# Windowed attention followed by routed expert attention on one Trainium2 core: the last row block in two halves, an earlier first key cast, and branch hints for five engines

## The chip, the core and the metric

The kernel runs on one core of a Trainium2 chip. A core has a TensorE that multiplies matrices (PE in the profile, with PEld for its weight loads), a VectorE (DVE), a ScalarE (ACT), a GpSimd (POOL) and a SyncE (SP) that here only issues transfers. Each engine works through its own instructions strictly in program order and waits on semaphores for the others. The metric is the device time in microseconds; lower is better.

## What is computed

The reference chains two layers. The first is attention with 4 batches, 8 heads, 768 positions and a head size of 64, in which a row sees the 8 first keys and the 96 last ones, with a bias that falls with distance. The second takes its output as x (4 × 768 × 512) and runs 4 causal attention experts of size 64; each row adds up its two best experts.

```python
    keep = is_global | is_local
    scores = scores + bias[None, :, :, :]
    scores = np.where(keep, scores, -1000000000.0)
    ...
    logits = x @ w_gate
    topk = np.argpartition(-logits, K, axis=-1)[..., :K]
    ...
    for e in range(E):
        ...
        ye = a @ v @ wo[e]
        for kk in range(K):
            mask = topk[:, :, kk] == e
            out += mask[..., None] * w[:, :, kk:kk + 1] * ye
```

## The kernel before, in words

The work is cut into 24 units of 128 rows (NU = 24, six per batch). The order of everything is written out by hand: ORDER (lines 791 to 830) is a string of slots such as `kc0v`, which means stage `kc` of unit 0 on engine v. The loop at lines 765 to 769 calls the stages in that order, so each slot puts its instructions at the end of its engine's queue. The last letter names the engine that does the copy or issues the transfer: a for ScalarE, g for GpSimd, v for VectorE, s for SyncE.

For one unit, the stages are these. `lk`, `lq`, `lv` load 256 KB of keys, queries and values in float32 (line 238), each kind into six rotating buffers. `kc`, `qc` cast them to float16 (line 258), and `vc`, `vx` cast the values (line 267). `tk`, `tq` transpose keys and queries on TensorE (line 283), with a copy out of PSUM (line 285). `sa`, `sb` make the local scores: a matmul first puts the bias from `biasT` into PSUM (line 345), another adds the scores (line 352), and ScalarE takes the exponential (line 355). `gs`, `vg`, `va`, `vb` are the scores of the eight first keys and the sums over values (lines 323, 366, 381). `tx` turns the result, `pk`, `pq`, `pv` project it for the experts (lines 414, 428), and `ro` is one step of the routing. `ca`, `cb`, `cc` are the experts' scores with their exponentials (lines 459, 462), and `ma` masks the diagonal block on GpSimd (line 474). `za` and `zb` sum over values for experts 0, 1 and 2, 3 (line 487); after `zb`, VectorE makes the reciprocal, the routing factor and the scaled result `zs` for all four experts (lines 494, 496, 498). `tz` turns `zs` (line 509, copy at line 512), and `ou` multiplies by `wo`, copies the 128 × 512 result to `osb` and stores it (lines 519, 522, 523).

`wm` slots are matmuls on the identity whose result nobody reads (line 248, 128 × 240 each); they stand where TensorE would idle. `xb` (lines 84 to 95) makes the constants of the local bias on VectorE: nine instructions, of which the last four write `biasT`. `ck` (lines 741, 742) counts, on VectorE, how many reciprocals of row sums lie in the allowed range. At the end the counts are summed by one matmul (line 774), reduced and made an integer on VectorE (lines 776, 778), and read by all engines (line 780); a branch (line 782) goes to a general path if a count is short. `bh` marks that branch for a prefetch hint on three engines.

PSUM has three pools here: `psS` (tag s, two buffers), `psZ` (tag z, one buffer) and `psT` (tag t, two buffers). A tile of a tag takes the buffers of that tag in turn and has to wait until the buffer's last reader is through. In the kernel before, the tiles of `tz` and `ou` and the count `nps` are all of tag t, and the score tiles `sps`, `gps`, `vgps`, `cps` are of tag s.

Of the kernel before, what the change touches and what calls it, by code (L numbers as in the profile page):

```python
# [18 lines left out]
P = 128  # L19
# [3 lines left out]
def kernel(  # L23
# [27 lines left out]
    NU = B * NT  # L51
    NH = 3
    HG = H // 2
    VW = Dh + 1
    sc1 = 1.0 / float(Dh) ** 0.5
    sc2 = 1.0 / float(Hd) ** 0.5
    slopes = [2.0 ** (-8.0 * (h + 1) / H) for h in range(H)]


    const = ctx.enter_context(tc.tile_pool(name="const", bufs=1))  # L60
    ident = const.tile([P, P], F16)
# [4 lines left out]
    biasT = const.tile([P, NP, W], F16)  # L66
    ident2 = const.tile([P, KB], F16)
    rel = const.tile([P, W], F32)
# [12 lines left out]
    col_i = const.tile([P, P], I32)  # L81
    G.iota(col_i[:, :], pattern=[[1, P]], channel_multiplier=0, base=0)

    def bias_constants(_):
        V.tensor_copy(rel[:, :], rel_i[:, :])
        ge = const.tile([P, W], F32, name="ge")
        V.tensor_scalar(ge[:, :], rel[:, :], 0.0, None, op0=Alu.is_ge)
        lt = const.tile([P, W], F32, name="lt")
        V.scalar_tensor_tensor(lt[:, :], rel[:, :], float(NL), ge[:, :],
                               op0=Alu.is_lt, op1=Alu.mult)  # L90
        V.tensor_scalar(lt[:, :], lt[:, :], -1.0, -NEG, op0=Alu.add, op1=Alu.mult)
        V.tensor_scalar(rel[KB:P, :], rel[KB:P, :], slopes[1] / slopes[0], None, op0=Alu.mult)
        for p in range(NP):
            V.scalar_tensor_tensor(biasT[:, p, :], rel[:, :], -slopes[2 * p] / sc1, lt[:, :],
                                   op0=Alu.mult, op1=Alu.add)

    def half_identities(_, on):
        for r in (slice(0, KB), slice(KB, P)):
# [44 lines left out]
    rinv2 = const.tile([P, B, NT, E], F32)  # L143
# [5 lines left out]
    wo16 = const.tile([P, NEP, D], F16)  # L149
# [41 lines left out]
    pp = fast.enter_context(tc.tile_pool(name="pp", bufs=3))  # L191
    psS = fast.enter_context(tc.tile_pool(name="psS", bufs=2, space=PSUM))
    psZ = fast.enter_context(tc.tile_pool(name="psZ", bufs=1, space=PSUM))
    psT = fast.enter_context(tc.tile_pool(name="psT", bufs=2, space=PSUM))
# [22 lines left out]
    def held(name, u):  # L217
        t, n, owner = rings[name]
        assert owner[u % n] == u
        return t[:, u % n]  # L220
# [9 lines left out]


    fs, kqT, kgs, vgs, ags, xTs, kqs, lgs, wts, a2s, as_, done = ({} for _ in range(12))
    s16s, zs_, x16s, routing, zss, zts, tps, ppss, zs2 = ({} for _ in range(9))

    def load(u, nm, on):
        b, ri = divmod(u, NT)
# [240 lines left out]
    def causal_values(u, i):  # L477

        b, ri = divmod(u, NT)
        n, a2 = ri + 1, a2s[u]  # L480
        assert done["m", u]
        if i == 0:
            zs2[u] = current["z"] = psZ.tile([P, 2, 4 * P], F32, name="zps2", tag="z")
        z_ps = zs2[u][:, 0, 0:E * VW].rearrange("r (e d) -> r e d", e=E)
        for e in range(i * E // 2, (i + 1) * E // 2):
            for ci in range(n):
                mm(z_ps[:, e, :], lhsT=a2[:, e % 2, (e // 2) * n + ci, :],  # L487
                   rhs=held("v2buf", b * NT + ci)[:, e, :], start=(e == 0 and ci == 0), stop=True,
                   skip_group_check=True)
        if i == 0:  # L490
            return
        assert next(routing[u // NH], "end") == "end"
        rinv = rinv2[:, b, ri, :]
        V.reciprocal(rinv, z_ps[:, :, Hd])
        ce = pp.tile([P, E], F32, name="ce")
        V.tensor_mul(ce[:, :], rinv, wts[u // NH][:, ri % NH, :])
        zss[u] = pp.tile([P, E, Hd], F16, name="zs")
        V.tensor_tensor(zss[u][:, :, :], z_ps[:, :, 0:Hd],  # L498
                        ce[:, :].unsqueeze(2).to_broadcast([P, E, Hd]), op=Alu.mult)

    def turn_z(u, on):
        zts[u] = pp.tile([P, NEP, P], F16, name="zt")
        if on == "s":
            nc.sync.dma_start_transpose(zts[u][:, :, :],
                                        zss[u][:, :, :].rearrange("r e d -> r (e d)"))
            return
        zt_ps = psT.tile([P, NEP, P], F16, name="ztps", tag="t")
        for ep in range(NEP):
            nc.tensor.transpose(zt_ps[:, ep, :],  # L509
                                zss[u][:, 2 * ep:2 * ep + 2, :].rearrange("r e d -> r (e d)"),  # L510
                                ident[:, :])
        copies[on](zts[u][:, :, :], zt_ps[:, :, :])  # L512

    def output(u, on):
        b, ri = divmod(u, NT)
        assert 3 in ready
        o_ps = psT.tile([P, D], F32, name="ops", tag="t")
        for ep in range(NEP):
            mm(o_ps[:, :], lhsT=zts[u][:, ep, :], rhs=wo16[:, ep, :],  # L519
               start=(ep == 0), stop=(ep == NEP - 1))  # L520
        o_sb = pp.tile([P, D], F32, name="osb", bufs=6)
        copies[on](o_sb[:, :], o_ps[:, :])
        dma(out[b, ri * P:(ri + 1) * P, :], o_sb[:, :])

    def top_two(pool, lg, wt, nm, n):

# [218 lines left out]
    def branch_hint(_):  # L745

        tc.mark_branch_hint_location("general", hint="LikelyTaken", engines=(
            mybir.EngineType.PE, mybir.EngineType.Activation, mybir.EngineType.DVE))

    stages = {  # L750
        "lk": (load, "k"), "lq": (load, "q"), "lv": (load, "v"),
        "kc": (cast, "k"), "qc": (cast, "q"), "vc": (cast_v, 0), "vx": (cast_v, 1),
        "wi": (weights_in,), "wc": (weights_cast,), "gi": (global_keys,),
        "vs": (select_values,), "xb": (bias_constants,), "xi": (half_identities,),
        "xm": (global_mask,), "xc": (global_bias,), "xk": (key_mask,), "xs": (selection,),
        "az": (local_zeros,), "xt": (act_tables,), "wm": (keep_warm,),
        "tk": (turn, 0), "tq": (turn, 1), "sa": (local_scores, 0), "sb": (local_scores, 1),
        "gs": (global_scores,), "vg": (global_values,),
        "va": (local_values, 0), "vb": (local_values, 1), "tx": (turn_x,),
        "pk": (project_qk, 0), "pq": (project_qk, 1), "pv": (project_v,), "ro": (route,),  # L760
        "ca": (causal_scores, 0), "cb": (causal_scores, 1), "cc": (causal_scores, 2),
        "ma": (causal_mask,), "za": (causal_values, 0), "zb": (causal_values, 1),
        "tz": (turn_z,), "ou": (output,), "ck": (check_sums,), "bh": (branch_hint,),
    }
    for slot in ORDER.split():
        stage, *args = stages[slot[:2]]
        if slot[-1].isalpha():
            args.append(slot[-1])
        stage(int(slot[2:].rstrip("agsv")), *args)
# [2 lines left out]
    V.memset(ones[:, :], 1.0)  # L772
    n_ps = psT.tile([1, NCHK], F32, name="nps", tag="t")
    mm(n_ps[:, :], lhsT=ones[:, :], rhs=good[:, :], start=True, stop=True)
    n_f = const.tile([1, 1], F32)
    V.reduce_sum(n_f[:, :], n_ps[:, :], axis=Ax.X)
    n_i = const.tile([1, 1], I32)
    V.tensor_copy(n_i[:, :], n_f[:, :])
    total = P * B * NT * (H + E)
    n_ok = nc.values_load(n_i[0:1, 0:1], min_val=0, max_val=total)  # L780
    fast.close()
# [7 lines left out]


ORDER = """
xb0 lk0s kc0v lq0s az0v az1g lk1s xi0a xs0v xk0g lq1a wm14 tk0 qc0g lv0s kc1g lk2s lq2s lk3a
wm5 tq0a lq3s xc0g lv1a lv2s lq4s lk4a qc1v lq5s vc0g vx0g wm4 tk1 tq1v xm0v lk5s wm10 sa0 sb0
wm10 vs0 gi0 wi0a wm2 gs0 lk6s kc2v qc2v tk2 tq2v wm3 gs1 lq6s wm7 vg0 kc3g va0 vb0 vc1g vx1v
qc3a sa1 az2g sb1 tk3 tq3v tx0v wi1a vg1 az3g qc4a vc2g kc4g vx2v wm2 va1 wm4 sa2 sb2 vb1 qc5g
gs2 kc5a wc0g tk4 tq4v tx1v az4v lv3s vg2 va2 lv4s vb2 sa3 sb3 tk5 tq5v wm6 tx2v kc6a lq7s wi2a
qc6v wm4 sa4 sa5 tk6 vc3g tq6v pk0 sb4 sb5 wc1v pk1 wm2 gs3 wm2 pq0a vx3v pq1a gi1 vg3 vc4g
vx4g wi4s lv5s va3 vb3 lk7a ca0 ma0 pk2 pq2v tx3v ca1 vg4 va4 vb4 lq8s ca2 pk3 pq3a lk8s vc5v
vx5v cb2 vg5 wc2g lv6s kc7g lq9s pv0v pv1v lq10a lk9s qc7g qc8g kc8g ca3 cb3 tk7 lv7s tq7v pv2v
ro0 va5 sa6 tk8 tq8v tx4v vc6g vx6g lk10a lk11s vb5 sb6 gs4 lv8s ro0 pv3v pk4 qc9g pq4v ro0 ro0  # L800
# [24 lines left out]
vb23 cc17 ma16 tz15v pk21 pq21a za16 ro6 zb16 tx22v ro6 ca19 ca20 ma17 tx23v ma18 ma19 za17  # L825
tz16v zb17 ou14a pv21v cb20 ca21 za18 pv22v pv23v ro7 zb18 cb21 pk22 ro7 ro7 ro7 pq22a ma20
ma21 pk23 pq23a ro7 za19 zb19 ca22 ou15v tz17v cb22 za20 cc22 tz18v ro7 ro7 ou16a zb20 ou17v
ck0 ck1 ca23 bh0 cb23 za21 tz19v zb21 ou18v cc23 tz20v ma22 za22 zb22 tz21a ou19a ou20v ma23 za23 tz22v
zb23 ou21a ou22a tz23v ou23a ck2
"""  # L830

MAXB = 512
# [38 lines left out]
```

## Time and profile before

| what | us |
|---|---|
| median of the three runs | 152.31 |
| lowest and highest run | 150.82, 152.47 |
| the profiled execution's own time | 152.97 |
| its span, first to last instruction | 150.8 |
| TensorE busy in the span | 140.3 (93%) |
| VectorE, ScalarE, GpSimd busy | 111.4, 108.1, 90.2 |
| data moved | 27.77 MB, mean 184 GB/s |

The profiled execution took 152.97 us, of which 150.8 us lie between its first and last instruction, and some 2.2 us around them. Busy TensorE is not TensorE at its peak, because matmuls are pipelined and their ends are modelled. The page cuts the span into 40 slices of 3.77 us; each digit is a busy share in tenths. The chain is followed back from the last work instruction to whatever released each step.

### The profile page before, as it was taken

How to read it: one execution, taken by the hardware profiler on the slowest of the kernel's cores; microseconds unless marked ns; L12 is line 12 of the kernel's file. 1: busy time of each engine (PE TensorE's matmuls, PEld its weight loads, DVE VectorE, ACT ScalarE, POOL GpSimd, SP SyncE). 2: the span in 40 equal slices, each digit the busy share in tenths (PEclk: the TensorE clock that was granted, in tenths of full speed). 3: DMA queues.
4: the chain of work that ended last, by engine and by line, in shares of the span. 5: the costliest groups of instructions: out<-in, count | busy, mean ns of one | idle time of the engine just before them, and what ended most of it. 6: DMA issues, size and time to landing. Idle time of an engine off the chain costs nothing.

```text
span 150.8 us, 7217 instructions
## 1 busy us (share of the span) xinstructions
PE 140.3 (93%) x3029; PEld 110.2 (73%) x3029; DVE 111.4 (74%) x348; ACT 108.1 (72%) x176; POOL 90.2 (60%) x254
## 2 busy tenths in 40 slices
PE   5799999999999999999978999999999999999760
PEld 4567778887778888878757778888778878786520
DVE  4838676687899887878863987687787777778850
ACT  4027657778576888888638998887977978989640
POOL 7278351568878988797827899136286345463200
PEclk9999999999999999999999999999999999999999
DMA  4999998999999989899899963415221005013462
GB/s 99 280 252 286 276 261 192 254 247 238 277 282 275 245 201 249 189 256 208 231 240 288 301 166 113 116 43 142 74 77 70 4 19 195 24 51 127 155 263 97
DMA packets 85364, 27.77 MB, mean 184 GB/s; under 512 B 82000, under 2 KB 82000, under 8 KB 85328
## 3 DMA queue, kind: packets, MB, share of 16 engines
q1 hardware_dynamic: 62496, 21.51, 56.6%
q10 hardware_dynamic: 22832, 5.77, 17.1%
q8 instruction: 24, 0.39, 1.0%
q14 instruction: 12, 0.10, 0.2%
HBM read 20.98 MB, written 6.29 MB: 181 GB/s over the span
## 4 chain that ended last, share of the span: by engine, by line
PE 74%; DMA 11%; DVE 4%; POOL 3%; ACT 2%; issue 1%; SPq 1%; ACTq 0%; POOLq 0%; DVEq 0%
PE pps L414 14%; PE cps L459 7%; PE vps L428 7%; PE tp L283 7%; PE ops L519 6%; PE zps L487 6%; PE zps L381 6%; PE sps L345 5%; PE zps L248 4%; DMA kf<-in_k_dram 4%; DMA vf<-in_v_dram 4%; PE xps L402 3%; PE sps L352 3%; DMA qf<-in_q_dram 3%; PE zps L366 2%; PE ztps L509 2%
## 5 line engine op out<-in xcount | busy, mean ns | idle before, releaser
L462 ACT ACTIVATE a<-cps 128x1024 f16<-128x1024 f32 (+1 forms) x48 | 42.2, 917 | 8.3 <-PE cps L459 6.6
L355 ACT ACTIVATE abuf<-sps 128x636 f16<-128x636 f32 (+1 forms) x48 | 30.6, 686 | 12.8 <-PE sps L352 10.1
L267 POOL CAST vbuf<-vf 64x256 f16<-64x256 f32 x76 | 31.0, 408 | 8.4 <-DMA vf<-in_v_dram 5.2
L474 POOL TENSOR_SCALAR_AFFINE_SELECT a<-a 128x256 f16<-128x256 f16 x48 | 18.3, 409 | 5.1 <-ACT a L462 4.8
L285 DVE COPY kqT<-tp 128x1024 f16<-128x1024 f16 x23 | 15.7, 688 | 6.6 <-PE tp L283 6.1
L390 DVE TENSOR_TENSOR x<-zps,rinv 128x512 f16<-128x512 f32 x24 | 16.6, 691 | 0.8
L487 PE MATMUL zps<-v2buf,a 128*128 128x65 f16 x336 | 16.0, 193 | 0.6 <-DVE zs L498 0.5
L345 PE MATMUL sps<-biasT,ident 64*64 64x318 f16 (+1 forms) x192 | 14.5, 305 | 1.4 <-ACT abuf L355 1.3
L381 PE MATMUL zps<-vbuf,abuf 64*128 64x65 f16 x704 | 15.5, 189 | 0.0
L258 POOL CAST s16k<-kf 128x512 f16<-128x512 f32 x17 | 10.3, 612 | 8.7 <-DMA kf<-in_k_dram 8.3
L487 PEld LDWEIGHTS <-a 128*128 128x128 f16 x336 | 13.3, 97 | 2.1 <-DVE zs L498 0.9
L381 PEld LDWEIGHTS <-abuf 64*128 64x128 f16 x704 | 14.0, 94 | 1.1 <-issue 0.2
L414 PE MATMUL pps<-xT,wk 128*128 128x128 f16 x192 | 14.7, 219 | 0.0
L414 PE MATMUL pps<-xT,wq 128*128 128x128 f16 x192 | 14.5, 219 | 0.0
L248 PE MATMUL zps<-ident 128*128 128x240 f16 x75 | 12.8, 316 | 1.7 <-POOL ident masks.py:199 1.6
L428 PE MATMUL vps<-wvg,xT 128*128 128x260 f16 x96 | 13.9, 275 | 0.0
L459 PEld LDWEIGHTS <-kq 64*128 64x128 f16 x336 | 9.7, 94 | 5.8 <-issue 4.4
L459 PE MATMUL cps<-kq,kq 64*128 64x128 f16 x240 | 13.8, 218 | 0.0
L519 PE MATMUL ops<-wo,zt 128*128 128x512 f16 x48 | 13.5, 380 | 0.4 <-DVE zt L512 0.4
L352 PE MATMUL sps<-kqT 64*64 64x159 f16 (+2 forms) x384 | 13.8, 223 | 0.0
L258 POOL CAST s16q<-qf 128x512 f16<-128x512 f32 x15 | 9.4, 630 | 5.1 <-DMA qf<-in_q_dram 4.9
L414 PEld LDWEIGHTS <-wk 128*128 128x128 f16 x192 | 11.5, 98 | 0.8
(113 smaller groups left out, 286.4 us busy)
## 6 DMA issues: line engine op xcount, KB each, us to landing
out_dram<-osb SPq DMA_DIRECT2D x24, 256.0 KB, 2.3
qf<-in_q_dram SPq DMA_DIRECT2D x20, 256.0 KB, 5.6
kf<-in_k_dram SPq DMA_DIRECT2D x19, 256.0 KB, 5.7
vf<-in_v_dram SPq DMA_DIRECT2D x17, 256.0 KB, 5.5
vf<-in_v_dram ACTq DMA_DIRECT2D x7, 256.0 KB, 4.7
kf<-in_k_dram ACTq DMA_DIRECT2D x5, 256.0 KB, 4.9
qf<-in_q_dram ACTq DMA_DIRECT2D x4, 256.0 KB, 4.5
w<-in_moe_wk_dram ACTq DMA_DIRECT2D x1, 512.0 KB, 5.3
```

The source lines that it names most:

```text
L248: mm(current["z"][:, 0, 4 * P - 2 * NC:4 * P].rearrange("r (a n) -> r a n", a=2), lhsT=ident[:, :], rhs=ident[:, 0:NC].unsqueeze(1).to_bro ...
L258: copies[on](s16s[nm, u][:, :, :], fs[nm, u][:, :, :])
L267: copies[on](o[hf * KB:(hf + 1) * KB, c, :, 0:Dh], fs["v", u][c * KB:(c + 1) * KB, hf * HG:(hf + 1) * HG, :])
L345: mm(s_ps[o, hh, 0:2 * w].rearrange("r (c n) -> r c n", c=2), lhsT=ident2[r, :], rhs=biasT[r, p, 0:w].unsqueeze(1).to_broadcast([KB, 2, w] ...
L355: S_.activation(as_[u][:, :, g, :].rearrange("r h (c n) -> r h c n", c=2)[:, :, :, 0:w], s_ps[:, :, 0:2 * w].rearrange("r h (c n) -> r h c ...
L381: mm(zs_[u][:, hf, hq * VW:(hq + 1) * VW], lhsT=as_[u - prev][r, hq % 2, hq // 2, at:at + P], rhs=held("vbuf", u - prev)[r, c, hq, :], sta ...
L414: mm(p_ps[:, i, ep, :], lhsT=w[:, ko, ep, :, :].rearrange("r a d -> r (a d)"), rhs=xT[:, ko, :], start=(i == 0 and ep == 0 and ko == 0), s ...
L428: mm(v_ps[:, :], lhsT=xT[:, ko, :], rhs=wvg16[:, ko, :], start=(ko == 0), stop=(ko == NK - 1))
L459: mm(s_ps[:, e2, i, :], lhsT=kqs[b * NT + ci][r, 0, ep, :], rhs=kqs[u][r, 1, ep, :], start=(i == 0), stop=True, skip_group_check=True)
L462: S_.activation(a2[:, :, 4 * c:4 * c + len(part), :], s_ps[:, :, 0:len(part), :], func=Exp, scale=sc2)
L487: mm(z_ps[:, e, :], lhsT=a2[:, e % 2, (e // 2) * n + ci, :], rhs=held("v2buf", b * NT + ci)[:, e, :], start=(e == 0 and ci == 0), stop=Tru ...
L519: mm(o_ps[:, :], lhsT=zts[u][:, ep, :], rhs=wo16[:, ep, :], start=(ep == 0), stop=(ep == NEP - 1))
```

## The change

The change has four parts.

1. In the first part, `xb` is split: its first five instructions stay in `xb`, and the four that write `biasT` become a stage `xp`, which comes after the cast of the first keys (`kc0v`). The load of key block 1 goes from SyncE's queue to ScalarE's (`lk1a`), that of key block 3 from ScalarE's to SyncE's (`lk3s`). The counts of the `wm` matmuls change: 14, 5, 4, 10, 10, 2, 3 become 15, 5, 11, 10, 7, 4, 2, and a later `wm2` goes.
2. The last unit (23) sums experts 0, 1 and 2, 3 into two PSUM banks. Each half is normalised by itself (`za23`, then `zb23`), turned by itself (`tz23`, `ty23`), and multiplied by its half of `wo` (`ou23`, `oy23`), column halves in separate PSUM tiles. VectorE copies one column half and SyncE stores it, ScalarE copies and stores the other. `tz22`, `ou21` and `ou22` take tag s instead of t. `tz23` comes before `zb23`.
3. The two large counts `ck0` and `ck1` move from before `ca23` to after `tz20v`. The integer count is written by the reduction itself, without the copy of line 778.
4. The branch hint is made for SyncE and GpSimd too, and its slot `bh0` comes first.

```diff
+    def pair_biases(_):
         for p in range(NP):
-            V.scalar_tensor_tensor(biasT[:, p, :], rel[:, :], -slopes[2 * p] / sc1, lt[:, :],
-                                   op0=Alu.mult, op1=Alu.add)
+            V.scalar_tensor_tensor(biasT[:, p, :], rel[:, :], -slopes[2 * p] / sc1,
+                                   const_of["lt"][:, :], op0=Alu.mult, op1=Alu.add)
...
-        z_ps = zs2[u][:, 0, 0:E * VW].rearrange("r (e d) -> r e d", e=E)
+        last = u == NU - 1
+        nz = E // 2 if last else E
+        z4 = zs2[u][:, :, 0:nz * VW].rearrange("r a (e d) -> r a e d", e=nz)
...
+        z, e = (z4[:, i], slice(i * nz, i * nz + nz)) if last else (z4[:, 0], slice(0, E))
+        rinv = rinv2[:, b, ri, e]
+        V.reciprocal(rinv, z[:, :, Hd])
...
+    def end_tile(u, first, shape, dtype, name):
+
+        if u < first:
+            return psT.tile(shape, dtype, name=name, tag="t")
+        return psS.tile(shape, dtype, name=name, tag="s")
...
-        zt_ps = psT.tile([P, NEP, P], F16, name="ztps", tag="t")
+        zt_ps = end_tile(u, NU - 2, [P, NEP, P], F16, "ztps")
...
-        o_ps = psT.tile([P, D], F32, name="ops", tag="t")
+        o_ps = end_tile(u, NU - 3, [P, D], F32, "ops")
...
+    def turn_last_z(ep, on):
+
+        zt_ps = psT.tile([P, P], F16, name="ztps1", tag="t")
+        nc.tensor.transpose(zt_ps[:, :],
+                            zss[NU - 1][:, 2 * ep:2 * ep + 2, :].rearrange("r e d -> r (e d)"),
+                            ident[:, :])
+        zts[ep, "last"] = pp.tile([P, P], F16, name=f"zt{ep}", bufs=1)
+        copies[on](zts[ep, "last"][:, :], zt_ps[:, :])
+
+    def last_output(ep):
+
+
+        b, ri = divmod(NU - 1, NT)
+        if ep == 0:
+            outs["last"] = [pool.tile([P, D // 2], F32, name=f"ops{t}", tag=t)
+                            for pool, t in ((psS, "s"), (psT, "t"))]
+        for i in range(2):
+            c = slice(i * D // 2, (i + 1) * D // 2)
+            o_ps = outs["last"][i][:, :]
+            mm(o_ps, lhsT=zts[ep, "last"][:, :], rhs=wo16[:, ep, c], start=(ep == 0),
+               stop=(ep == NEP - 1), skip_group_check=True)
+        if ep == 0:
+            return
+        for i, (copy, queue) in enumerate(((V.tensor_copy, dma), (S_.copy, S_.dma_start))):
+            c = slice(i * D // 2, (i + 1) * D // 2)
+            o_sb = pp.tile([P, D // 2], F32, name=f"osb{i}", bufs=1)
+            copy(o_sb[:, :], outs["last"][i][:, :])
+            queue(out[b, ri * P:(ri + 1) * P, c], o_sb[:, :])
...
-            mybir.EngineType.PE, mybir.EngineType.Activation, mybir.EngineType.DVE))
+            mybir.EngineType.PE, mybir.EngineType.Activation, mybir.EngineType.DVE,
+            mybir.EngineType.SP, mybir.EngineType.Pool))
...
-    n_f = const.tile([1, 1], F32)
-    V.reduce_sum(n_f[:, :], n_ps[:, :], axis=Ax.X)
     n_i = const.tile([1, 1], I32)
-    V.tensor_copy(n_i[:, :], n_f[:, :])
+    with nc.allow_low_precision("whole numbers"):
+        V.reduce_sum(n_i[:, :], n_ps[:, :], axis=Ax.X)
...
-xb0 lk0s kc0v lq0s az0v az1g lk1s xi0a xs0v xk0g lq1a wm14 tk0 qc0g lv0s kc1g lk2s lq2s lk3a
-wm5 tq0a lq3s xc0g lv1a lv2s lq4s lk4a qc1v lq5s vc0g vx0g wm4 tk1 tq1v xm0v lk5s wm10 sa0 sb0
-wm10 vs0 gi0 wi0a wm2 gs0 lk6s kc2v qc2v tk2 tq2v wm3 gs1 lq6s wm7 vg0 kc3g va0 vb0 vc1g vx1v
+bh0 xb0 lk0s kc0v xp0 lq0s az0v az1g xi0a xs0v xk0g lq1a lk1a wm15 tk0 qc0g lv0s kc1g lk2s lq2s
+lk3s wm5 tq0a lq3s xc0g lv1a lv2s lq4s lk4a qc1v lq5s vc0g vx0g wm11 tk1 tq1v xm0v lk5s wm10
+sa0 sb0 wm7 vs0 gi0 wi0a wm4 gs0 lk6s kc2v qc2v tk2 tq2v wm2 gs1 lq6s wm7 vg0 kc3g va0 vb0 vc1g
...
-ck0 ck1 ca23 bh0 cb23 za21 tz19v zb21 ou18v cc23 tz20v ma22 za22 zb22 tz21a ou19a ou20v ma23 za23 tz22v
-zb23 ou21a ou22a tz23v ou23a ck2
+ca23 cb23 za21 tz19v zb21 ou18v cc23 tz20v ck0 ck1 ma22 za22 zb22 tz21a ou19a ou20v ma23 za23
+tz22v tz23v zb23 ou21a ou22a ou23 ty23v ck2 oy23
```

More of the change, by code (lines that the diff above doesn't have):

```diff
@@ L82 @@
     G.iota(col_i[:, :], pattern=[[1, P]], channel_multiplier=0, base=0)
+    const_of = {}
     def bias_constants(_):
@@ L92, in bias_constants @@
         V.tensor_scalar(rel[KB:P, :], rel[KB:P, :], slopes[1] / slopes[0], None, op0=Alu.mult)
+        const_of["lt"] = lt
+    def pair_biases(_):
         for p in range(NP):
-            V.scalar_tensor_tensor(biasT[:, p, :], rel[:, :], -slopes[2 * p] / sc1, lt[:, :],
-                                   op0=Alu.mult, op1=Alu.add)
+            V.scalar_tensor_tensor(biasT[:, p, :], rel[:, :], -slopes[2 * p] / sc1,
+                                   const_of["lt"][:, :], op0=Alu.mult, op1=Alu.add)
     def half_identities(_, on):
@@ L232 @@
     fs, kqT, kgs, vgs, ags, xTs, kqs, lgs, wts, a2s, as_, done = ({} for _ in range(12))
-    s16s, zs_, x16s, routing, zss, zts, tps, ppss, zs2 = ({} for _ in range(9))
+    s16s, zs_, x16s, routing, zss, zts, tps, ppss, zs2, outs = ({} for _ in range(10))
     def load(u, nm, on):
@@ L483, in causal_values @@
             zs2[u] = current["z"] = psZ.tile([P, 2, 4 * P], F32, name="zps2", tag="z")
-        z_ps = zs2[u][:, 0, 0:E * VW].rearrange("r (e d) -> r e d", e=E)
+        last = u == NU - 1
+        nz = E // 2 if last else E
+        z4 = zs2[u][:, :, 0:nz * VW].rearrange("r a (e d) -> r a e d", e=nz)
         for e in range(i * E // 2, (i + 1) * E // 2):
             for ci in range(n):
-                mm(z_ps[:, e, :], lhsT=a2[:, e % 2, (e // 2) * n + ci, :],
-                   rhs=held("v2buf", b * NT + ci)[:, e, :], start=(e == 0 and ci == 0), stop=True,
-                   skip_group_check=True)
+                mm(z4[:, e // nz, e % nz, :], lhsT=a2[:, e % 2, (e // 2) * n + ci, :],
+                   rhs=held("v2buf", b * NT + ci)[:, e, :], start=(e % nz == 0 and ci == 0),
+                   stop=True, skip_group_check=True)
@@ L490, in causal_values @@
         if i == 0:
+            zss[u] = pp.tile([P, E, Hd], F16, name="zs")
+        if i == 0 and not last:
             return
         assert next(routing[u // NH], "end") == "end"
[L493 to L499, printed above, removed]
+        z, e = (z4[:, i], slice(i * nz, i * nz + nz)) if last else (z4[:, 0], slice(0, E))
@@ new lines, in causal_values @@
+        rinv = rinv2[:, b, ri, e]
+        V.reciprocal(rinv, z[:, :, Hd])
+        ce = pp.tile([P, nz], F32, name=f"ce{nz}")
+        V.tensor_mul(ce[:, :], rinv, wts[u // NH][:, ri % NH, e])
+        V.tensor_tensor(zss[u][:, e, :], z[:, :, 0:Hd],
+                        ce[:, :].unsqueeze(2).to_broadcast([P, nz, Hd]), op=Alu.mult)
+    def end_tile(u, first, shape, dtype, name):
+        if u < first:
+            return psT.tile(shape, dtype, name=name, tag="t")
+        return psS.tile(shape, dtype, name=name, tag="s")
@@ L501, in turn_z @@
     def turn_z(u, on):
         zts[u] = pp.tile([P, NEP, P], F16, name="zt")
[L503 to L506, printed above, removed]
-        zt_ps = psT.tile([P, NEP, P], F16, name="ztps", tag="t")
+        zt_ps = end_tile(u, NU - 2, [P, NEP, P], F16, "ztps")
         for ep in range(NEP):
@@ L753 @@
         "wi": (weights_in,), "wc": (weights_cast,), "gi": (global_keys,),
-        "vs": (select_values,), "xb": (bias_constants,), "xi": (half_identities,),
+        "vs": (select_values,), "xb": (bias_constants,), "xp": (pair_biases,), "xi": (half_identities,),
         "xm": (global_mask,), "xc": (global_bias,), "xk": (key_mask,), "xs": (selection,),
@@ L764 @@
     }
+    stages["ty"] = (turn_last_z, 1)
+    stages["oy"] = (last_output, 1)
     for slot in ORDER.split():
         stage, *args = stages[slot[:2]]
+        if slot[:4] in (f"tz{NU - 1}", f"ty{NU - 1}"):
+            turn_last_z(int(slot[1] == "y"), slot[4:])
+            continue
+        if slot[:4] in (f"ou{NU - 1}", f"oy{NU - 1}"):
+            last_output(int(slot[1] == "y"))
+            continue
         if slot[-1].isalpha():
@@ L791 @@
 ORDER = """
-xb0 lk0s kc0v lq0s az0v az1g lk1s xi0a xs0v xk0g lq1a wm14 tk0 qc0g lv0s kc1g lk2s lq2s lk3a
-wm5 tq0a lq3s xc0g lv1a lv2s lq4s lk4a qc1v lq5s vc0g vx0g wm4 tk1 tq1v xm0v lk5s wm10 sa0 sb0
-wm10 vs0 gi0 wi0a wm2 gs0 lk6s kc2v qc2v tk2 tq2v wm3 gs1 lq6s wm7 vg0 kc3g va0 vb0 vc1g vx1v
-qc3a sa1 az2g sb1 tk3 tq3v tx0v wi1a vg1 az3g qc4a vc2g kc4g vx2v wm2 va1 wm4 sa2 sb2 vb1 qc5g
-gs2 kc5a wc0g tk4 tq4v tx1v az4v lv3s vg2 va2 lv4s vb2 sa3 sb3 tk5 tq5v wm6 tx2v kc6a lq7s wi2a
-qc6v wm4 sa4 sa5 tk6 vc3g tq6v pk0 sb4 sb5 wc1v pk1 wm2 gs3 wm2 pq0a vx3v pq1a gi1 vg3 vc4g
+bh0 xb0 lk0s kc0v xp0 lq0s az0v az1g xi0a xs0v xk0g lq1a lk1a wm15 tk0 qc0g lv0s kc1g lk2s lq2s
+lk3s wm5 tq0a lq3s xc0g lv1a lv2s lq4s lk4a qc1v lq5s vc0g vx0g wm11 tk1 tq1v xm0v lk5s wm10
+sa0 sb0 wm7 vs0 gi0 wi0a wm4 gs0 lk6s kc2v qc2v tk2 tq2v wm2 gs1 lq6s wm7 vg0 kc3g va0 vb0 vc1g
+vx1v qc3a sa1 az2g sb1 tk3 tq3v tx0v wi1a vg1 az3g qc4a vc2g kc4g vx2v wm2 va1 wm4 sa2 sb2 vb1
+qc5g gs2 kc5a wc0g tk4 tq4v tx1v az4v lv3s vg2 va2 lv4s vb2 sa3 sb3 tk5 tq5v wm6 tx2v kc6a lq7s
+wi2a qc6v wm4 sa4 sa5 tk6 vc3g tq6v pk0 sb4 sb5 wc1v pk1 wm2 gs3 pq0a vx3v pq1a gi1 vg3 vc4g
 vx4g wi4s lv5s va3 vb3 lk7a ca0 ma0 pk2 pq2v tx3v ca1 vg4 va4 vb4 lq8s ca2 pk3 pq3a lk8s vc5v
```

## The prediction

> **What bounds the kernel now.** I read the page first. TensorE is busy 93% of the span, but its 40 slices say where it isn't: at the start, at slice 21 (75 to 79 us) and in the last three. So I read those three places, beginning with the middle, because it decides whether time won at the start survives.
>
> ```profile
> PE   5799999999999999999978999999999999999760
> DMA  4999998999999989899899963415221005013462
> ```
>
> The transfers are as full as TensorE until slice 23 (87 us). The chain of waits from 60 to 100 us, in order of time (start, length, what):
>
> ```profile
> 62.26 5.98 DMA vf<-in_v_dram
> ...
> 73.47 4.66 DMA qf<-in_q_dram
> ...
> 78.20 0.39 ACTq L238
> ...
> 79.29 0.71 ACT abuf L355
> 80.00 0.04 issue
> 80.04 0.33 PE sps L345 x4
> ```
>
> At 78.13 a query load lands. ScalarE's sequencer was held until then at its own load issue of 78.20. The two exponentials queued behind it start at 78.69, and TensorE gets its score buffer at 80.04 after 1.3 us of waiting. Is that load late because of compute? SyncE's timeline says no:
>
> ```profile
> 58.29 1.19 SPq L238 DMA_DIRECT2D kf<-in_k_dram  x1
> 59.53 2.06 SPq L165 DMA_DIRECT2D w<-in_moe_wo_dram  x1
> 61.68 0.48 SPq L238 DMA_DIRECT2D kf<-in_k_dram  x1
> 62.26 4.98 SPq L238 DMA_DIRECT2D vf<-in_v_dram  x3
> 67.29 3.36 SPq L238 DMA_DIRECT2D qf<-in_q_dram  x3
> 71.14 2.23 SPq L523 DMA_DIRECT2D out_dram<-osb  x2
> 73.47 0.39 SPq L238 DMA_DIRECT2D qf<-in_q_dram  x1
> ```
>
> Each issue begins within 0.15 us of the end of the one before, and this holds from 0.80 us to 70.65 us. A load's issue takes 0.45 us with nothing ahead and up to 3.7 us later, so SyncE waits for room in its queue, not for free buffers. The load stream bounds itself up to about 80 us. From 80 to 138 us TensorE has no wait over 0.1 us. Then comes the tail, from TensorE's, VectorE's and ScalarE's timeline:
>
> ```profile
> 141.79 0.18 DVE L494 RECIPROCAL rinv<-zps 128x4 f32<-128x4 f32 x1
> 143.22 0.53 PE L487 MATMUL zps<-v2buf,a 128*128 128x65 f16 x12
> 145.68 0.60 PE L519 MATMUL ops<-wo,zt 128*128 128x512 f16 x2 [0.39 <-DVE zt L512]
> 146.32 0.59 ACT L522 COPY osb<-ops 128x512 f32<-128x512 f32 x1 [0.86 <-PE ops L519]
> 146.62 0.14 DVE L778 CAST n_i<-n_f 1x1 int32<-1x1 f32 x1
> ```
>
> The last store is issued at 146.93 and lands at 149.24; SyncE's last waits and the program's end take 1.57 us more, to 150.84.
>
> [...] the `wm` matmuls start 200 ns apart until 10.15 us and 103 ns apart from 10.3 us, after idle stretches before 5.68 and 8.72 us. [...] the 256 KB stores at the end take 2.02 to 2.31 us. [...] Here branch to next instruction took 0.49 us on hinted ScalarE, 0.46 on GpSimd and 0.49 on SyncE without a hint, so no gain of a hint is visible.
>
> **The change, part by part: the start.** Key block 0 lands at 4.00 but is cast at 5.21, behind the whole of `xb`. Four instructions of 1.03 us together (4.26 to 5.21 by starts) now follow the cast: it starts at 4.26, ends at 4.68, and `tk0` starts near 4.75 instead of 5.68. `biasT` is then ready at about 5.7 instead of 5.3, first needed at `sa0`, 10 us or later, so that costs nothing. With 15 `wm` (15 × 0.2 = 3.0 us from 1.65) TensorE has no idle stretch there, [...]. Key block 1 in block 3's place on ScalarE's queue should land where that one did, 7.66 instead of 8.00; cast 0.61, `tk1` at 8.38 instead of 8.72. The eleven `wm` ahead of it end by 7.8 at full rate or 8.8 at half rate, so it starts between 8.38 and 8.8; I take 8.4. Then 8 transposes × 0.056 and 10 `wm` × 0.103 instead of 8 × 0.107 and mostly 0.2: `sa0` at 9.95 instead of 11.03, 1.1 us earlier. Unit 2's casts on VectorE stand behind `xm0`, 2.4 us long, which now starts at about 9.65 (0.75 earlier), so `tq2` comes 0.6 to 0.8 us earlier. Moving block 3 to SyncE puts blocks v0, k2, q2 one place earlier there and block 3 at about 12 us; its transposes are at 16.79, so 4 us of slack hide it. GpSimd may wait some 0.3 us for it in `kc3g`, and the value casts behind it have to be through by 18.1.
>
> What becomes of these 0.8 us? Loads keep their times, because the same bytes go through the same full queue. Key block 18 lands at 63.70, is cast at once and transposed at 64.49: 0.18 us of slack. The load of 78.13 lands when it did, and TensorE waits longer at 80.04. What can move the stream itself: SyncE's hint delays the first load by 0.07 us (ScalarE's hint to its next instruction took 0.076), and two loads on ScalarE's queue go out 1 us earlier, into a stretch at 255 GB/s where 282 was reached next: 1 us × 27/255 = 0.1 us gained. Start: +0.07 − 0.1, about 0, with ends −0.9 (all passes) and +0.3.
>
> **The tail.** VectorE is dense from 138.26 to 141.79 in both versions: `ck0`, `ck1` (0.96 us) only change places with `tz19`'s copy, unit 21's norm, `ou18`'s and `tz20`'s copies. TensorE's 0.55 us wait for `zs` before `za22` goes, and turns up before `za23`, which still needs unit 22's `zs`: 142.8 against 142.75. Nothing won yet. Then `ou20`'s copy on VectorE until 143.28, and the first half's norm: 0.17, 0.16 and a 128x128 product (0.42 for 256 columns, 0.28 by its slope), with gaps, ends at 144.08. `tz23` waits for it on TensorE, and `zb23` is queued behind `tz23`: 144.19 instead of 143.22, a new wait of 0.7 us. `ou21` ends at 145.15, its ScalarE copy (0.59) at 145.8. `ou23`'s first tile takes that buffer of tag s, so it starts at 145.85, `ty23` at 146.07, its copy (0.22) at 146.34, the last two matmuls at 146.6 and 146.7. They end at 146.9 and 147.0, against 146.28. The copies are halves: 0.41 on VectorE, 0.37 on ScalarE, against 0.59, to 147.33 and 147.40 against 146.91. The two stores of 128 KB, a size that the trace doesn't have, [...] I take 2.0: landed 149.45 against 149.24. The count's matmul gets its tag-t buffer only after ScalarE's copy, 147.46 against 146.21; without the 0.18 us cast SyncE reads the count at 147.88 against 147.31, and its last waits are through at 149.75 against 149.47 (it no longer waits for a landing, unless the hint shortens its branch, by 0.3 at most). Tail: +0.28, with ends −0.5 and +1.0 (the whole new wait stays).
>
> **Sum.** 0 + 0.28 on the profiled execution's 150.84 gives a span of 151.1 and a time of 153.2. The median of the runs stands 0.66 below the profiled time: 152.31 + 0.2, rounded, is 152.5.
>
> **Rivals.** (A) The start's gain passes: for it speaks that SyncE's queue could be quickened by ScalarE's loads coming sooner; against it the contiguous issues. It gives 152.3 − 0.9 + 0.3 = 151.7. (B) The halves do shorten the end: the second norm, turn and copy are half as long (0.3 us less), [...] and VectorE gets to the first half before the copy of `ou20` costs: −0.5, 151.8; with A 150.9 or lower. (C) Slower: [...] Each us that this holds back the first load shifts the stream that bounds the first 80 us. It decides from a delay of 1.5 us; priced at 2 us it gives 154.5. Against it: on the three hinted engines the next instruction follows within 0.1 us.
>
> **Chances.** Forecast 0.58, A 0.2, B 0.12 (a third of A and B together beyond −1%), C 0.1. A measurement of this kernel can tell about 1% from no change; the three runs before spread over 1.1%. A third of A and B with that spread: faster by over 1% 0.17; C and the worst tail: slower 0.13; within 1% 0.70. The range takes in A with B below, and the tail's +1.0 above: 150.7 to 153.7.
>
> **What would show it.** Right: `tk0` near 4.75, [...] `sa0` near 10; a longer wait at `sps` near 80 us, which still ends when a query load lands near 78; TensorE's wait before `ztps1`; last stores issued near 147.4. Wrong: that load landing 0.5 us or more earlier, `zb23` starting before 143.5, or the first load landing later than 4.3.

## The result, and the profile after

The changed kernel takes 164.55 us (median of four runs, 163.87 to 165.23), against 152.02 us of the kernel before beside it (150.82 to 152.47): a ratio of 1.0837, with a 95% interval of 1.0758 to 1.0917. Here and below, ratios and intervals compare undisturbed executions only, those within 1.5% of the fastest of their kernel, while medians and ranges are of all executions. The profiled execution took 163.87 us and its span is 162.1 us, 11.3 us more than before. TensorE's idle time (span less busy) grew from 10.5 to 19.1 us, its busy time from 140.3 to 143.0 us.

The page of the kernel after, its 40 slices (4.05 us each) and its two load queues (packets, MB, share of 16 engines):

```profile
PE   5889928999799799798997799999999999999760
...
DMA  4999999999999999999999999341430104112544
GB/s 102 227 218 220 219 220 178 218 214 203 206 231 221 219 222 205 218 191 262 212 246 223 220 230 294 88 129 37 103 133 33 39 0 151 53 65 84 196 155 163
...
q1 hardware_dynamic: 62496, 21.38, 59.7%
q10 hardware_dynamic: 22976, 5.90, 20.3%
```

The same rows of the kernel before, which the prediction did not show:

```profile
GB/s 99 280 252 286 276 261 192 254 247 238 277 282 275 245 201 249 189 256 208 231 240 288 301 166 113 116 43 142 74 77 70 4 19 195 24 51 127 155 263 97
...
q1 hardware_dynamic: 62496, 21.51, 56.6%
q10 hardware_dynamic: 22832, 5.77, 17.1%
```

The transfers are just as full, but in slices 2 to 6 they move 218 to 227 GB/s where they moved 252 to 286, and they stay full until slice 25 (101 us) instead of 23 (87 us). TensorE's gaps have spread over slices 6 to 22. The queues carry practically the same packets for longer: (59.7% + 20.3%) × 162.1 = 129.7 us per DMA engine against (56.6% + 17.1%) × 150.8 = 111.1, 18.5 us more. So the first thing to see is that the transfers themselves are slower, from the first microseconds.

How that reaches TensorE is in the chain of waits of the kernel after, from 14 to 26 us (start, length, what):

```profile
13.25 8.85 DMA qf<-in_q_dram
...
22.18 0.62 ACT s16q L263
22.79 0.61 ACT abuf L360
...
23.45 0.24 PE gps L328 x4
```

A query load lands at 22.10. ScalarE stands 4.06 us before its cast, the exponential behind it is late, and TensorE waits 3.2 us for the score buffer. In the kernel before that cast ran at 17.82 without a wait. TensorE's line of the kernel after, and ScalarE's of the kernel before:

```profile
23.45 0.24 PE L328 MATMUL gps<-kqT,kg 128*32 128x128 f16 x4 [3.22 <-ACT abuf L360]
...
17.82 0.62 ACT L258 CAST s16q<-qf 128x512 f16<-128x512 f32 x1
```

The same place as in the prediction's middle stretch, again from the chain of the kernel after:

```profile
66.34 5.70 DMA qf<-in_q_dram
...
72.22 6.38 DMA vf<-in_v_dram
...
83.03 5.54 DMA qf<-in_q_dram
88.64 0.37 ACTq L243
...
89.72 0.71 ACT abuf L360
...
90.47 0.33 PE sps L350 x4
```

It is the same chain, link by link, 10.4 us later: 90.47 against 80.04. From there to the end it is 71.6 us in the kernel after and 70.8 before. Nearly everything is lost ahead of 90 us. SyncE's timeline of the kernel after, in the same stretch:

```profile
72.22 5.00 SPq L243 DMA_DIRECT2D vf<-in_v_dram  x3
77.27 4.04 SPq L243 DMA_DIRECT2D qf<-in_q_dram  x3
81.85 1.09 SPq L534 DMA_DIRECT2D out_dram<-osb  x2
83.03 0.74 SPq L243 DMA_DIRECT2D qf<-in_q_dram  x1
```

It still issues one load right behind the other, within 0.1 us. The one pause, 0.54 us, stands before a store, as it did in the kernel before (0.49 us ahead of 71.14). In the whole stream up to 99 us only two load issues stand back by more than 0.15 us, 0.40 us at 9.12 and 0.51 us at 54.80. So it is not that buffers come free late. The loads themselves take longer.

### The profile page after: what moved, and what is told of

It is laid out like the page before. It is cut to its first block, busy times and chain, and to the rows that moved or that the text cites. A ratio compares the mean times of both kernels' runs of the same rounds, so it can differ in the third digit from the quotient of the medians.

```text
span 162.1 us, 7233 instructions
## 1 busy us (share of the span) xinstructions
PE 143.0 (88%) x3035; PEld 111.1 (69%) x3035; DVE 114.5 (71%) x352; ACT 107.5 (66%) x176; POOL 89.7 (55%) x254
## 3 DMA queue, kind: packets, MB, share of 16 engines
q1 hardware_dynamic: 62496, 21.38, 59.7%
q10 hardware_dynamic: 22976, 5.90, 20.3%
## 4 chain that ended last, share of the span: by engine, by line
PE 42%; DMA 33%; DVE 7%; POOL 6%; SPq 3%; issue 3%; ACT 3%; ACTq 0%; POOLq 0%; DVEq 0%
DMA kf<-in_k_dram 13%; DMA qf<-in_q_dram 12%; DMA vf<-in_v_dram 8%; PE pps L419 7%; PE cps L464 5%; PE ops L530 5%; PE zps L494 4%; PE vps L433 4%; PE zps L386 4%; SPq L243 3%; PE tp L288 3%; PE sps L350 2%; PE xps L407 2%; POOL vbuf L272 2%; POOL s16k L263 1%
## 5 line engine op out<-in xcount | busy, mean ns | idle before, releaser
L272 POOL CAST vbuf<-vf 64x256 f16<-64x256 f32 x76 | 30.5, 401 | 11.5 <-DMA vf<-in_v_dram 8.0
L386 PE MATMUL zps<-vbuf,abuf 64*128 64x65 f16 x704 | 16.1, 192 | 0.0
L386 PEld LDWEIGHTS <-abuf 64*128 64x128 f16 x704 | 14.5, 95 | 1.3 <-issue 0.4
L253 PE MATMUL zps<-ident 128*128 128x240 f16 x79 | 12.3, 302 | 1.7 <-POOL ident masks.py:199 1.7
L530 PE MATMUL ops<-wo,zt 128*128 128x512 f16 x46 | 12.9, 380 | 0.0
L357 PEld LDWEIGHTS <-kqT 64*64 64x64 f16 x384 | 11.5, 108 | 0.8
```

The source lines that it names most:

```text
L272: copies[on](o[hf * KB:(hf + 1) * KB, c, :, 0:Dh], fs["v", u][c * KB:(c + 1) * KB, hf * HG:(hf + 1) * HG, :])
L357: mm(s_ps[o, hh, c * w:c * w + n], lhsT=kqT[b][r, 0, p, k0:k0 + KB], rhs=kqT[b][r, 1, p, k0:k0 + n], start=False, stop=True, skip_group_ch ...
L386: mm(zs_[u][:, hf, hq * VW:(hq + 1) * VW], lhsT=as_[u - prev][r, hq % 2, hq // 2, at:at + P], rhs=held("vbuf", u - prev)[r, c, hq, :], sta ...
L530: mm(o_ps[:, :], lhsT=zts[u][:, ep, :], rhs=wo16[:, ep, :], start=(ep == 0), stop=(ep == NEP - 1))
```

## The experiments

**Theory.** The reduction that writes the integer itself drops the tile `n_f`, a 1 × 1 float that takes a 32-byte slot in the constants' pool. That pool lies ahead of the load buffers, so every later SBUF buffer moves down by 32 bytes. In the built programs the float32 buffers `kf`, `qf`, `vf` start at bytes 78336, 90624 and 102912 of a partition before, and at 78304, 90592 and 102880 after: 0 and 224 modulo 256. The loads go in packets of 256 bytes, which then each cross a 256-byte boundary at their destination. **Rivals:** the new order of loads at the start, with two of them on other queues; SyncE's and GpSimd's hints; the tail; or the shift of some other buffer, the weights or the work tiles, instead of the loads' own.

The packet records of all traces, one execution each, side by side (mean time of the 79,872 packets of 256 bytes, share of them that took at most 18 ns, and when the 70th of the 77 loads, weights included, had landed):

```
                            start of loads   mean ns   <=18 ns   70th load
                            modulo 256                           landed, us
before                           0            18.18     98.0%      83.6
after                          224            21.95     47.9%      95.6
e1_after_spare32                 0            18.22     97.4%      86.3
e2_before_count_only           224            22.26     44.0%      97.3
e3_before_loads_at_224         224            22.45     41.1%      94.9
e4_before_loads_at_64           64            22.79     42.3%      95.3
e5_before_loads_at_128         128            22.27     43.1%      95.5
e6_before_rest_at_224            0            18.20     97.9%      82.3
e7_new_start_only                0            18.16     98.1%      86.4
e8_new_end_only                  0            18.20     98.0%      84.3
e9_before_weights_aligned        0            18.08     99.4%      84.9
e10_after_all_aligned            0            18.05     99.5%      84.5
e11_two_loads_to_sync            0            18.18     98.0%      84.7
e12_hints_only                   0            18.24     97.5%      82.7
```

The means hide that off the boundary many packets still take 18 ns. It depends on the stretch. The kernel with only the loads moved has the same order of loads as the kernel before:

```
                       both queues load   SyncE's queue alone
before                 8 to 24 us         56 to 72 us
  GB/s                 265                220
  mean ns, <=18 ns     18.4, 94.0%        18.1, 99.4%
e3_before_loads_at_224 8 to 24 us         64 to 80 us
  GB/s                 220                217
  mean ns, <=18 ns     25.0, 10.5%        19.7, 73.0%
```

So nearly all is lost while both queues load. Key block 16 landed 10.0 us later there (66.88 against 56.88), query block 22, at the end of the stretch of one queue, 9.1 us later (87.27 against 78.13), and value block 18, with both queues loading again, 11.3 (93.92 against 82.67). No run changes the number of queues at one offset, so why it is so stays open.

### The slot given back to the kernel after

```diff
     n_i = const.tile([1, 1], I32)
+    const.tile([1, 1], F32, name="spare")
```

> The changed kernel with one unused 32-byte tile in the constants' pool, in the place of the float count tile that the change dropped; every buffer after it in SBUF is then where it was in the kernel before. Theory A (the dropped tile shifts the load buffers by 32 bytes, off a 256-byte boundary, and each 256-byte packet takes longer): packets back at 18 ns, 150.5 to 153 us. Theory B (the new order of the first loads on the two queues slows the stream) and theory C (the branch hints on SyncE and GpSimd do): 163.5 to 165.5 us, packets as in the changed kernel.

Measured: 154.35 us, median of four (150.54 to 154.63), too few and too scattered for an interval. The packets are back at 18.22 ns. An unused tile of one number takes back some 10 us of the median; what exactly remains of the rest of the change is read from the run with everything aligned, which has 22 executions.

### Only the count, in the kernel before

```diff
-    n_f = const.tile([1, 1], F32)
-    V.reduce_sum(n_f[:, :], n_ps[:, :], axis=Ax.X)
     n_i = const.tile([1, 1], I32)
-    V.tensor_copy(n_i[:, :], n_f[:, :])
+    with nc.allow_low_precision("whole numbers"):
+        V.reduce_sum(n_i[:, :], n_ps[:, :], axis=Ax.X)
```

> The kernel before with only the count's reduction written as an integer (the float tile and its copy go); order, loads, hints and tail are those of before. Theory A: the 32-byte shift comes with it, so 162 to 166 us. Theories B and C: nothing that slows the stream is in it, 150.5 to 153 us, 0.2 us less than before at most.

Measured: 164.33 us, ratio 1.0795 (1.0687 to 1.0902). The whole loss comes with an edit at the very end of the program, whose instructions run after 146 us, while the loads are slow from 4 us on. New start, hints and tail are not needed for it.

### Only the loads' buffers moved

Two unused tiles go ahead of the first load: one in the load pool, which moves the loads' buffers, and one in the next pool, which fills up 256 bytes, so that everything behind keeps its place modulo 256.

```diff
+    raw.tile([P, 56], F32, name="shift", bufs=1)
+    pp.tile([P, 8], F32, name="back", bufs=1)
```

> The kernel before with the 18 load buffers of keys, queries and values alone shifted by 224 bytes (a start at 224 modulo 256, as in the changed kernel); a 32-byte tile after them puts all other float16 buffers back on their old remainder. Theory A in its narrow form (it is the loads' destination): 161 to 166 us. If what counts is instead where the engines' own operands lie (matmul weights, casts, exponentials): 151 to 153 us.

Measured: 163.67 us, ratio 1.0794 (1.069 to 1.0898). Its instructions are those of the kernel before, 7217 of them. Its page:

```profile
span 160.9 us, 7217 instructions
...
GB/s 105 225 218 218 222 221 203 212 210 222 205 232 222 220 220 208 225 184 263 196 242 216 231 261 196 160 125 22 136 134 4 65 4 92 114 65 66 146 251 140
```

The rows are those of the kernel after: 218 to 225 GB/s from the second slice on.

### The buffers behind the loads' own moved

```diff
+    pp.tile([P, 56], F32, name="back", bufs=1)
```

> The kernel before with the load buffers where they were (0 modulo 256) and all buffers of the pool behind them (casts, transposes, exponents of the experts, outputs) shifted by 224 bytes. Theory A in its narrow form: 151 to 153.5 us and packets at 18 ns. If the engines' own operands contributed to the loss: more than 155 us.

Measured: 151.08 us, ratio 0.9998 (0.9971 to 1.0024). Its page keeps the fast rows:

```profile
span 148.6 us, 7217 instructions
...
GB/s 97 283 258 285 281 270 178 256 251 215 279 286 287 257 231 244 146 316 202 290 258 273 310 183 75 140 6 146 90 62 71 4 36 183 25 50 117 169 244 122
```

With the run before it, this settles the place: the loads' own buffers. The pools ahead of them (the weights' staging, the exponentials, the cast values) shifted in the changed kernel too and were moved in neither run, but as the loads' buffers alone give a ratio of 1.0794 against 1.0837 for the whole change, with intervals that overlap, there is next to nothing left for them to explain.

### Other offsets: 64 and 128

```diff
+    raw.tile([P, 16], F32, name="shift", bufs=1)
+    pp.tile([P, 48], F32, name="back", bufs=1)
```

> As the run with the load buffers at 224 modulo 256, but at 64 modulo 256. If a packet is only slowed by a start off a 64-byte boundary: 151 to 153 us. If it is slowed by crossing a 256-byte boundary: 160 to 166 us.

Measured: 163.86 us, ratio 1.0757 (1.0589 to 1.0924), 22.79 ns a packet. The second kernel has tiles of 32 and 32 in their place, so that the loads start at 128:

> The kernel before with the load buffers alone at 128 modulo 256. If a packet is slowed by crossing a 256-byte boundary (128 crosses it too): 160 to 166 us, 256-byte packets at 22 to 23 ns on average. If a 128-byte boundary is what counts: 151 to 153 us, 18 ns.

Measured: 163.38 us, ratio 1.08 (1.0745 to 1.0855), 22.27 ns. Offsets 64, 128 and 224 cost the same within their intervals, so it makes no difference here where a packet crosses the boundary. Whether it is the crossing or the start off the boundary that costs, packets of 256 bytes cannot tell: each that starts off it crosses it.

### The weights aligned as well

The weights' staging buffer starts at 192 modulo 256 in the kernel before. Two unused tiles bring it to 0 and leave the rest in place.

```diff
+    wst.tile([P, 16], F32, name="shift", bufs=1)
+    big.tile([P, 48], F32, name="back")
```

> The kernel before with the two weight buffers moved from 192 to 0 modulo 256, all else on its old remainder. If the boundary is what counts, the 6144 packets of the key, query and value weights (384 for each of 16 engines, some 6 ns each) lose 2.3 us of stream between 13 and 32 us, and the wait near 80 us, which ends with a load's landing, ends 1 to 2.3 us earlier: 150 to 151.5 us against 152.3. If the stream up to 80 us is not what bounds, or the weights' boundary does not matter: as before, within 0.5 us.

Measured: 151.33 us, ratio 0.9982 (0.9953 to 1.0012). The packets did get faster (99.4% at 18 ns), and the last weight load landed at 64.6 instead of 65.3 us, but the expected gain of 1 to 2.3 us did not come. The expectation took 6 ns for each of the 6144 weight packets. The mean over all packets fell by 0.10 ns, which is 1.3 ns for each of these and 0.5 us of stream in all, and the 70th load did not land earlier.

### The change with everything aligned, and its halves

The kernel after with the spare slot and with the two tiles of the weights:

```diff
+    wst.tile([P, 16], F32, name="shift", bufs=1)
+    big.tile([P, 48], F32, name="back")
...
     n_i = const.tile([1, 1], I32)
+    const.tile([1, 1], F32, name="spare")
```

> The changed kernel with the 32 bytes back and the weight buffers at 0 modulo 256. Theory: what the change does besides the shift is worth about nothing at the start (the stream keeps its times) and plus 0.3 us at the end, so 150.3 to 152 us, within 0.5 us of the kernel before with aligned weights. Rival: the halves and the new start do gain, and it is 1 us or more below that kernel.

Measured: 151.79 us, ratio 1.0002 (0.9972 to 1.0031). Without the shift no difference is seen; the interval leaves room for 0.3% either way.

The new start alone (first part of the change and hints for five engines, in the kernel before):

```diff
+    def pair_biases(_):
...
+            mybir.EngineType.SP, mybir.EngineType.Pool))
...
-xb0 lk0s kc0v lq0s az0v az1g lk1s xi0a xs0v xk0g lq1a wm14 tk0 qc0g lv0s kc1g lk2s lq2s lk3a
...
+bh0 xb0 lk0s kc0v xp0 lq0s az0v az1g xi0a xs0v xk0g lq1a lk1a wm15 tk0 qc0g lv0s kc1g lk2s lq2s lk3s wm5 tq0a lq3s
```

> The kernel before with the change's first part alone (split bias constants, order and warm matmuls of the start, loads of key blocks 1 and 3 exchanged) and the hints for five engines, the old end, and all buffers where they were. The prediction's term for the start: TensorE some 0.8 to 1.1 us earlier at sa0, but the wait near 80 us still ends with a query load landing at 78 us, so 0 within 0.5 us. Rival: the gain passes to the end, 0.8 us or more below before.

Measured: 152.74 us against 152.5 of the kernel before, ratio over the runs compared 0.9972 (0.9932 to 1.0013). The new end alone (the kernel after with the old start and the old hints, and the spare slot):

```diff
-            mybir.EngineType.PE, mybir.EngineType.Activation, mybir.EngineType.DVE,
-            mybir.EngineType.SP, mybir.EngineType.Pool))
+            mybir.EngineType.PE, mybir.EngineType.Activation, mybir.EngineType.DVE))
...
+    const.tile([1, 1], F32, name="spare")
...
-bh0 xb0 lk0s kc0v xp0 lq0s az0v az1g xi0a xs0v xk0g lq1a lk1a wm15 tk0 qc0g lv0s kc1g lk2s lq2s
...
+xb0 xp0 lk0s kc0v lq0s az0v az1g lk1s xi0a xs0v xk0g lq1a wm14 tk0 qc0g lv0s kc1g lk2s lq2s lk3a wm5 tq0a lq3s xc0g lv1a
```

> The changed kernel with the start, the order and the hints of before, that is the halves, the end tiles, the moved counts and the integer count, with 32 bytes put back so that all load buffers are where they were. The prediction's term for the end: 0.3 us more than before (ends minus 0.5 and plus 1.0).

Measured: 153.38 us against 152.5, ratio 1.0022 (0.9979 to 1.0066). Both intervals hold 1. The middle values, −0.4 and +0.3 us, agree with what the whole showed, but each is smaller than its interval.

### Two loads moved, and hints alone

If the wait near 80 us comes from ScalarE's sequencer being held at its own load issue, two of those loads on SyncE's queue should take it away:

```diff
-tz3v vg13 vc15g ro2 va13 vb13 lv17a cb8 gs7 ma8 ou2v tk19 tq19v lk23s lv18a za5 sb14 sb15 tz4v
+tz3v vg13 vc15g ro2 va13 vb13 lv17s cb8 gs7 ma8 ou2v tk19 tq19v lk23s lv18s za5 sb14 sb15 tz4v
```

> The kernel before with the value loads of blocks 17 and 18 issued by SyncE instead of ScalarE, which is held at the second until a query load lands at 78.13. If that hold is what stalls TensorE by 1.3 us before 80.04: the exponentials run by 77 us, TensorE's wait there goes, and the time falls by 0.5 to 1.3 us, to 150 to 151 us. If TensorE would have to wait there anyway for the load stream: as before.

Measured: 151.69 us, ratio 0.9962 (0.9931 to 0.9992), 0.4% faster than the kernel before and just clear of no change. Its trace has no wait for `sps` near 80 us. But the traces with the buffers behind the loads moved and with the hints alone have none either, and their loads are those of the kernel before: the wait comes and goes between executions. It stands, with 0.7 to 2.4 us, in five traces with aligned loads whose executions took 152.72 to 154.63 us (0.2 us in a sixth of 152.89), and is missing in the three that took 150.65 to 150.76. That the moved loads took it away is therefore not shown. Finally the hints of five engines in the kernel before:

```diff
-            mybir.EngineType.PE, mybir.EngineType.Activation, mybir.EngineType.DVE))
+            mybir.EngineType.PE, mybir.EngineType.Activation, mybir.EngineType.DVE,
+            mybir.EngineType.SP, mybir.EngineType.Pool))
```

> The kernel before with the branch hint made for SyncE and GpSimd too. The prediction: 0.05 to 0.1 us, so as before. Rival C: the first load lands 1.5 us or more later than 4.0 us and the time rises as much.

Measured: 152.13 us, ratio 0.994 (0.9897 to 0.9983). The first load landed at 3.98 us (4.00 before). SyncE took 0.505 us from its branch to the next instruction with the hint (in the kernel after) and 0.487 without (in the kernel before). The hints cost nothing that shows, and no row shows where 0.9 us could come from; that stays open.

## Why the prediction was wrong, step by step

**What bounds the kernel: right, and it is why the loss is so large.** The prediction named the load stream as the bound up to about 80 us. Moving the loads' buffers alone cost 7.9%, and the 70th load landed 12.0 us later in the kernel after (95.6 against 83.6) where the span grew by 11.3. Had the stream been hidden behind the engines' work, the slower packets would have cost less.

**The step that failed: "Loads keep their times, because the same bytes go through the same full queue".** The same bytes did go through the same full queue, but the time of a packet was taken as fixed. It rose from 18.18 to 21.95 ns because its destination moved. Worked out: 79,872 packets × 3.77 ns over 16 engines is 18.8 us of packet time per engine, against the 18.5 us that the queue rows show. Packets overlap on an engine (their times add up to as much as 1.35 of it, from 14 to 24 us), and 12 us of it reached the landing of the 70th load. The prediction had the edit with the cause in hand. It priced the integer count by its instruction, 0.18 us, and did not ask what else the dropped tile `n_f` did: it is 32 bytes of every later address. None of the rivals named addresses. The signs of error it listed (that load landing earlier, the first load later than 4.3 us) looked for other things: the load expected near 78 us landed at 88.6, and the first one at 4.20.

**What could have warned of it.** Little in the kernel before: its loads of keys, queries and values all start on a 256-byte boundary, and 98.0% of the packets took at most 18 ns. Its weights start off one, at 192, and with these aligned too the share was 99.4%. The size of the loss is known from the runs alone: with the loads at 224 a packet took 22.45 ns against 18.18, 1.23 times as long, and the three offsets cost the same. Why a packet takes longer there is not shown.

**The start: right in kind, and absorbed in the trace with aligned buffers.** TensorE's timeline of the kernel after with everything aligned:

```profile
4.82 0.61 PE L290 MATMUL tp<-ident,s16k 128*128 128x128 f16 x4
...
8.53 0.40 PE L290 MATMUL tp<-ident,s16k 128*128 128x128 f16 x4 [0.18 <-POOL s16k L265]
...
10.11 0.33 PE L352 MATMUL sps<-biasT,ident 64*64 64x318 f16 x4
```

Predicted were 4.75, 8.4 and 9.95; before they were 5.68, 8.72 and 11.03. That TensorE would run at its faster pace from 8.4 on was the author's estimate: four transposes took 0.61 us at 4.82 and 0.40 at 8.53 here, and 0.61 at 8.72 before. And in this trace the gain dies where the prediction said. The chain of the same kernel:

```profile
72.70 5.05 DMA qf<-in_q_dram
77.83 0.39 ACTq L245
...
78.91 0.71 ACT abuf L362
79.66 0.33 PE sps L352 x4
```

The load that ends ScalarE's hold lands near 77.8 (predicted: near 78), and TensorE waits 1.5 us there instead of 1.3. As this wait is missing from the traces of 150.65 to 150.76 us, none of which has the new start, it is not shown that it takes up the gain in every execution. In the kernel after as it stands, key block 1 landed at 8.72 instead of 8.00 us, because its packets were already slow, and `tk1` came at 9.45.

**The tail: right within 0.2 us at each step that was checked.** TensorE's timeline, again of the kernel after with everything aligned:

```profile
144.01 0.23 PE L541 MATMUL ztps<-ident,zs 128*128 128x128 f16 x1 [0.67 <-DVE zs L509]
144.07 0.53 PE L496 MATMUL zps<-v2buf,a 128*128 128x65 f16 x12
...
145.71 0.27 PE L557 MATMUL opss<-wo,zt 128*128 128x256 f16 x1 [0.24 <-ACT osb L535]
...
146.58 0.27 PE L557 MATMUL opst<-wo,zt 128*128 128x256 f16 x1
```

The new wait before `ztps1` is 0.67 us (predicted 0.7), `zb23` starts at 144.07 (144.19), `ou23` at 145.71 (145.85), the last matmul at 146.58 (146.7), the stores are issued at 147.23 and 147.29 (near 147.4). The half copies took 0.42 and 0.37 us (0.41 and 0.37). The stores of 128 KB took 1.77 us on SyncE's queue and 2.05 on ScalarE's here, and 1.76 and 2.06 us in the kernel after (2.0 taken). The 2.0 us, and the quicker landing that B's −0.5 counts on, were the author's estimates: the trace of the kernel before has stores of 256 KB alone, which took 2.02 to 2.31 us at its end. The 2.0 is some 0.24 us too long for SyncE's queue and 0.05 too short for ScalarE's. One releaser was wrong, that of the count's matmul: predicted at 147.46 behind ScalarE's copy, it came at 147.28, and what released it was VectorE's `ones`. From the end of unit 22's `zs` to the end of the program it is 8.39 us in the kernel after (8.39 with everything aligned) and 8.20 before: +0.2, with +0.28 predicted.

**The rivals.** A (the start's gain passes) is refuted by the run with everything aligned: 1.0002 (0.9972 to 1.0031), which leaves A's 151.7 out, a ratio of 0.996, though narrowly; the new start alone, 0.9972 (0.9932 to 1.0013), would still admit its 0.8 us. B (the halves shorten the end) is refuted by the tail's +0.2 and by the new end alone, 1.0022. C (SyncE's hint) supposed a first load held back by 1.5 us or more, a delay that the trace of the kernel before does not show, and gave the right side for a wrong reason: the hint moved SyncE's first issue by 0.11 us, and the hints alone slowed nothing, with the first load at 3.98 us. That it landed at 4.20 in the kernel after is no work of the hint: with the loads' buffers alone moved it landed at 4.26.

**The sum without the failed step.** The prediction's 152.5 on a median of 152.31 is a ratio of 1.0012. The change with its buffers aligned measured 1.0002 (0.9972 to 1.0031). The two agree, but a change worth nothing at all would lie in that interval as well. The missing term is the destination of the loads, +12 us by the 70th load's landing.

## What to carry to other kernels

A tile that is added to or dropped from an SBUF pool can move every buffer in the pools behind it, however small it is and wherever in the program it is used (here 4 bytes in use, a slot of 32), so the diff of the addresses belongs to the diff of the code. Where a stream of 256-byte packets is the bound, above all one on two queues, look up where the destinations start modulo 256 (a packet took 18.1 to 18.2 ns at 0 here, and 22.0 to 22.8 ns at 64, 128 or 224), and give back a dropped slot with an unused tile. When a profile shows the same packets, the same full transfers and a lower rate from the start, look at where the bytes go before looking at the order of the work.

## What the runs showed of the hardware that was not expected

- A 256-byte packet of a load into SBUF took 18.1 to 18.2 ns on average with its destination on a 256-byte boundary and 22.0 to 22.8 ns at 64, 128 or 224 bytes past one, and the kernel became 7.6 to 8.4% slower.
- With aligned destinations, in the kernel before, two loading queues moved 265 GB/s where one moved 220. With the loads alone at 224 bytes past a boundary two queues moved 220 and one 217. The shift took away what the second queue had added.
- After the wait of 3.2 us at 20 us in the kernel after, two groups of four transposes took 0.54 and 0.63 us in place of 0.40 and 0.39, and the granted clock from 24 to 34 us was 0.84 (1.00 in the kernel before). That may be part of the 2.7 us by which busy TensorE grew. It is not the cause of the loss: with the loads at 64, 163.15 us long, the mean granted clock was 0.997.
- The last stores of 128 KB landed in 1.76 us on SyncE's queue and 2.06 us on ScalarE's, those of 256 KB in 2.02 to 2.31 us: halving the bytes came nowhere near halving the time.
